# A two-block kernel in one program: in the first tile, two transposes of k and three blocks of w_out's roundings change their places

## The chip, the cores and the metric

The kernel runs on one core of a Trainium2 chip. The time is the device time of that core in microseconds (us), as the median of the runs. TensorE is PE in the profile (its weight loads are PEld), VectorE is DVE, ScalarE is ACT, GpSimd is POOL, and SyncE, which here only issues DMAs, is SP. ACT and POOL issue DMAs too.

## The reference

Two blocks follow each other. The first is a retention block with decay over 8 batches, 8 heads, 576 positions and 64 columns a head; the second is a gated feed-forward block (SwiGLU).

```
scores = q @ k.T / 8                           # per batch and head, 576 x 576
x      = (scores * decay[head]) @ v            # decay: gamma_h ** (i - j) for i >= j, else 0
x      = x.transpose(0, 2, 1, 3).reshape(4608, 512)
g      = x @ w_gate                            # 512 x 1536
out    = (g * sigmoid(g) * (x @ w_val)) @ w_out   # w_out: 1536 x 512
```

## The kernel before

Attention is done in chunks of 64 positions, for pairs of heads: 8 batches of 4 pairs are 32 pairs, numbered through; HP is 4. The 4608 tokens are cut into a first tile of 512 tokens (tile 0) and four tiles of 1024. Tiles 1 to 4 multiply their matrices with a scheme of fewer block products and more block sums; the sums fall to DVE and POOL. Tile 0 multiplies plainly.

The order of each engine's instructions is the order in which the program writes them: a manual schedule holds for all five engines. So where a line stands in the program decides what waits behind what.

**Tile 0, up.** In `plan` (lines 1513 to 1547) twelve steps f = 0 to 11 make one block of 128 hidden columns each, by `up0(f, ...)` (859): 4 products with w_gate into one PSUM bank and 4 with w_val into a second, then a silu of the first on ACT (874) and a product of the two on DVE (875). Even steps use bankA and bankB, odd ones bankC and bankE. So step f+2 overwrites the banks that step f's silu and product read. The profile counts each fp32 matmul twice, so a step's bank is a row of x8.

**Weights.** They arrive as float64 and are made float32 in two halves per block. `load_w` (368) issues a load of 1 MB, the later ones on POOL's queue. `split(j)` (389) is two ACT instructions (398, 399) that split the halves' bits, into one of two pairs of buffers; `rounding(j)` (408) is two DVE instructions (415, 416) that put them together, and then issues `split(j + 1)`. A split after the second half of a block issues the load of the block three further on (402 to 406). The blocks' order is `order` (361): blocks 0 to 11 are w_gate and w_val in turn, blocks 12 to 17 are w_out, with 12 between 6 and 7, 13 between 8 and 9, and 14 between 10 and 11. `round_until(i)` (1515) puts all roundings up to block i into the plan. The blocks that step f needs are rounded two steps ahead; those of w_out are needed only by tile 0's down stage (`down0`, 880), after all steps.

**Ticks.** Between the steps stand ticks, one per pair of heads. `tick(t)` (787) writes PE's attention products for pairs t-1 and t-2 and then a list `pieces`: copies on ACT, x of pair t-2 on DVE or ACT, masks and states of pair t-1 on DVE, and last, from `transposes(t)` (455), the DVE transposes of q and of k of pair t (line 477, into qT and the single buffer kT). `end_masks` (691) ends the pieces of tick 6. Without `spread` a tick runs all its pieces at once; `go_on(n)` (839) runs the next n. Tick 5 stands behind step 3, tick 6 behind step 5, tick 7 behind step 7, ticks 8 and 9 behind steps 10 and 11. PE's products of tick t+1 read what the transposes of tick t made. `end_transposes` (680, two DVE instructions on line 682) prepares the rest of batch 0, which PE reads in tick 6 (688).

**Loads of q, k and v.** `load(t)` (255) issues 10 DMAs for a pair on SP's queue: k and v by tokens (290), q and k again for the transposes (299), 4 each. SP issues in order.

**After the steps** come tile 0's down stage, with ticks 10 to 13 and with the sums of w_out's blocks on DVE and POOL (904), stored by SP (974, named dn); then tile 1, in which POOL makes the weight sums (1061) that PE reads (1208).

Of the kernel before, what the change touches and what calls it, by code (L numbers as in the profile page):

```python
# [132 lines left out]
def kernel(  # L133
# [38 lines left out]
    HP = H // 2  # L172
# [71 lines left out]
    def whole(i):  # L244

        return HP <= i < needed(2) - 2
# [262 lines left out]
    def own_values(i, n=0):  # L509

        s, ret = st[i], places(i)[0]
        cs = [a + d for a in (1 - n, 5 - n) for d in (0, 2)] if whole(i) else range(0 if n else NC - 1)
        for c in cs:
            for hl in range(2):
                rows, at = chunk(i, hl, c)
                start = n == 0 and c in (cs[:2] if whole(i) else (0, 1))
                m = nc.tensor.matmul(value(i, hl, c), s["v"][rows, at], ret[rows, c % 2 if whole(i) else hl, c // 2],  # L517
                                     start=start, stop=start, skip_group_check=True)
        if n == 0:
            s["own"] = m  # L520

    def new_states(i):
        s = st[i]
        for c in range(NFULL):
            for r in range(2):
                for hl in range(2):
                    rows, at = chunk(i, hl, 2 * c + r)
                    nc.tensor.matmul(z[half[hl], r, c], s["kn"][chunk(i, hl, 2 * c + r)], s["v"][rows, at],  # L528
                                     start=True, stop=True, skip_group_check=True)

    def earlier_values(i):
        s, (_, ret_last, state) = st[i], places(i)

        wait = nc.tensor.nop()
        tc.add_manual_dep(wait.ins, s["own"].ins.name,
                          mybir.DependencyInfo(mybir.DependencyClass.Sync, mybir.DependencyReason.DATA), reason="row halves")
        own_values(i, 1)
        for hl in range(0 if i < HP else 2):
            rows, at = chunk(i, hl, NC - 1)
            nc.tensor.matmul(xr[half[hl]], s["v"][rows, at], ret_last[rows],  # L540
                             start=False, stop=False, skip_group_check=True)
        for c in (1, 3, 4, 6, 5, 7, 2, 8) if whole(i) else range(1, NC - (i < HP)):
            for hl in range(2):
                nc.tensor.matmul(xr[half[hl]] if c + 1 == NC else value(i, hl, c), state[half[hl], c, :],  # L544
                                 s["qT"][half[hl], ts(c, L)], start=False, stop=True, skip_group_check=True)
# [140 lines left out]
    def end_scores():  # L686
        for n, x, hl in ends:
            nc.tensor.matmul(end_at[x][half[hl ^ x], n], end_k[half[hl], 2 * x + n], end_q[half[hl], 2 * x + n],
                             start=False, stop=True, skip_group_check=True)
# [5 lines left out]
    def end_own(x):  # L695
        for n, _, hl in [e for e in ends if e[1] == x]:
            rows = half[hl ^ x]
            m = nc.tensor.matmul(end_at[x][half[hl ^ x], n], end_v[rows, 2 * x + n], end_ret[rows, 2 * x + n],
                                 start=False, stop=False, skip_group_check=True)
        return m  # L700

    def end_earlier():
        for n, x, hl in ends:
            nc.tensor.matmul(end_at[x][half[hl ^ x], n], end_states[half[hl], 2 * x + n], end_q[half[hl], 2 * x + n],
                             start=False, stop=True, skip_group_check=True)
# [7 lines left out]
    pieces = []  # L713
# [73 lines left out]
    def tick(t, lo=HP, hi=NP, spread=False, then=None):  # L787
        go_on(len(pieces))
        if lo <= t - 2 < hi:
            own_values(t - 2)  # L790
            if t == HP + 3:
                st[t - 2]["own"] = end_own(1)
        if lo <= t - 1 < hi:
            new_states(t - 1)
        if lo <= t - 2 < hi:
            earlier_values(t - 2)
            if t == HP + 3:
                end_own(0)
                end_earlier()
        if lo <= t - 1 < hi:  # L800
            scores(t - 1, t - 2 < lo)
            if t == HP + 2:
                end_scores()
        if lo <= t - 1 < hi and whole(t - 2) and not whole(t - 1):
            decay(slice(0, H), slice(0, H), half[1])
        copies, *masks = masked(t - 1) if lo <= t - 1 < hi else (lambda: None,)
        keys, *new = transposes(t) if lo <= t < hi else (lambda: None,)
        outputs = to_x(t - 2)[0] if lo <= t - 2 < hi else lambda: None
        late = needed(1) - 4 <= t < needed(1) - 2 or light(t - 2)
        if late and masks:  # L810
            own, (last, pairs, odd, evens) = masks
            pieces.extend([lambda: (copies(), own(), outputs()), [last, pairs, odd, lambda: (evens(), keys())]])
        elif late:
            pieces.append(lambda: (copies(), outputs(), keys()))
        else:
            pieces.extend([lambda: (copies(), keys()), outputs])
            for own, (last, pairs, *rest_of) in [masks] if masks else []:
                pieces.extend([own, [lambda: (last(), pairs()), *rest_of]])
        if then and new:
            pieces.extend(new[:-1])  # L820
            pieces.append(lambda: (new[-1](), then()))
        else:
            pieces.extend(new)
            pieces.extend([then] if then else [])
        if t == HP + 2:
            pieces.append(end_masks)
        if t == HP + 3:
            pieces.append(end_to_x)
        if not spread:
            go_on(len(pieces))  # L830
# [8 lines left out]
    def go_on(n):  # L839
        for _ in range(min(n, len(pieces))):  # L840
            while part_on():
                pass
# [16 lines left out]
    def up0(f, chunks, parts=range(2)):  # L859

        pair = banks[2 * (f % 2) : 2 * (f % 2) + 2]
        for gv in parts:
            bank = pair[gv]
            for c in chunks:
                w = w_up[:, f // 4, gv, f % 4, c // 2, (c % 2) * P : (c % 2 + 1) * P]
                if f == 2 or f == 3 and gv == 0:
                    for m in range(2):
                        nc.tensor.matmul(bank[:, ts(m, TB)], w, xs[0][:, c, ts(m, TB)],
                                         start=(c == 0 and m == 0), stop=(c == HP - 1), skip_group_check=True)
                    continue  # L870
                last_up[0] = nc.tensor.matmul(bank, w, xs[0][:, c, :], start=(c == 0), stop=(c == HP - 1))  # L871
        if HP - 1 in chunks:
            s = io[:, (f % 2) * T0 : (f % 2 + 1) * T0]
            nc.scalar.activation(out=s, in_=pair[0], func=AF.Silu)
            nc.vector.tensor_tensor(out=hid0[f], in0=pair[1], in1=s, op=ALU.mult)
# [629 lines left out]
    FIRST = needed(1) - 2  # L1505
# [7 lines left out]
    plan = []  # L1513

    def round_until(i):
        while todo and order.index(i) >= todo[0]:
            m = todo.pop(0)
            plan.extend(lambda j=j: rounding(j, j != 2 * len(order) - 3) for j in (2 * m, 2 * m + 1))

    round_until(3)  # L1520
    tick_at = {2: 4, 3: 5, 5: 6, 7: 7, 10: 8, 11: 9}
    for f in range(2, NF):
        if f == 3:
            plan.append(lambda: tick(HP, HP, FIRST))
        round_until({4: 12, 6: 13, 8: 14, 9: 15, 10: 16, 11: 17}.get(f, f + 2))
        last_half = plan.pop() if f + 1 == NF else None
        plan.append(lambda f=f: up0(f, range(HP)))
        if last_half:
            plan.append(last_half)
        if f + 2 == NF:  # L1530
            plan.append(lambda: split(2 * len(order) - 2))
        if f + 1 == NF:
            plan.append(lambda: pool_places.extend(wide_places))
            plan.append(negate)
        if f - 1 in tick_at and f < 7:
            plan.append(lambda t=tick_at[f - 1]: next_load(t))
        if f in tick_at and f > 2:
            plan.append(lambda t=tick_at[f]: tick(t, HP, FIRST))
            if tick_at[f] == HP + 1:
                plan.append(end_transposes)  # L1540
        if f in (7, 10):
            if f == 10:
                plan.append(lambda: next_load(9))
            plan.append(lambda t=tick_at[f]: next_load(t))
# [3 lines left out]
    tick_at = {1: 10, 3: 11, 6: 12, 8: 13}  # L1548
# [89 lines left out]
```

## Time and profile before

| what | value |
|---|---|
| runs before | 1015.73 us median; 1012.75, 1015.73, 1017.21 |
| profiled execution, its own time | 1016.05 us |
| its span in the profile | 1014.3 us |
| granted TensorE clock, mean | 0.998 |
| PE busy | 1003.5 us |
| DVE busy | 721.5 us |
| POOL busy | 576.7 us |
| ACT busy | 285.7 us |
| DMA | 194.44 MB, 192 GB/s mean |

The page gives shares of the whole span. The views used below go closer: the table by stage gives, for a stretch of time, each engine's busy time with its instructions in brackets, the granted clock and the DMA share; the timeline gives each instruction's start, its length, its engine and line, what it writes and reads, and in square brackets how long its engine stood idle before it and what ended that; the chain of waits follows the work that ended last back through what released it. The queue shares list the packets, the megabytes and the share of the 16 DMA engines of each DMA queue: q0 carries POOL's loads, q1 what SP issues.

### The profile page before, as it was taken

Reading aid. Unit: us, or ns where it says so; the run is one execution under the profiler, and the core shown is the slowest. Engines: PE = TensorE matmul, PEld = TensorE weight load, DVE = VectorE, ACT = ScalarE, POOL = GpSimd, SP = SyncE. Lnnn points to the kernel's source line nnn. Section 1 sums busy time; section 2 is a strip of 40 time slices with the busy share of each in tenths; the row PEclk is TensorE's granted clock in tenths of the full one; section 3 lists DMA queues with packets and bytes.
Section 4 is the critical chain, followed back from the end, with each engine's and each line's share of the span. In section 5 each row is a group of like instructions: output and inputs, shape, how many; then the busy total and the mean of one; then the engine's idle time right before and its main releaser. Section 6 shows DMA issues by size and latency. Waiting matters only on the chain.

```text
span 1014.3 us, 21283 instructions
## 1 busy us (share of the span) xinstructions
PE 1003.5 (99%) x8302; PEld 827.2 (82%) x8302; DVE 721.5 (71%) x1210; ACT 285.7 (28%) x636; POOL 576.7 (57%) x611
## 2 busy tenths in 40 slices
PE   8989999999999999999999999999999999999998
PEld 6644555888888888888888888888888888888887
DVE  5549889578886675977778678866575767566745
ACT  5535632132423322133322202233320012233110
POOL 3511348989577218575564157746672586566614
PEclk9999999999999999999999999999999999999999
DMA  9999977788788886857668786434454454445553
GB/s 235 272 221 300 200 202 276 199 227 224 147 232 248 211 185 218 206 170 199 185 180 226 172 200 191 163 126 166 161 172 141 147 195 146 145 152 186 176 162 103
DMA packets 273933, 194.44 MB, mean 192 GB/s; under 512 B 212329, under 2 KB 241897, under 8 KB 273833
## 3 DMA queue, kind: packets, MB, share of 16 engines
q1 hardware_dynamic: 249448, 99.49, 39.9%
q10 hardware_dynamic: 20208, 79.57, 24.1%
q0 software_dynamic: 4176, 14.03, 4.2%
q8 instruction: 66, 1.08, 0.5%
q14 instruction: 35, 0.28, 0.1%
HBM read 154.11 MB, written 38.93 MB: 190 GB/s over the span
## 4 chain that ended last, share of the span: by engine, by line
PE 93%; SPq 3%; DMA 2%; ACT 0%; issue 0%; DVE 0%; ACTq 0%; DVEq 0%
PE bankB L1208 12%; PE bankE L1208 12%; PE bankA L1208 12%; PE bankC L1208 12%; PE bankE L1415 7%; PE bankC L1415 7%; PE bankB L1415 7%; PE bankA L1415 6%; SPq L299 2%; PE outer L517 2%; PE inner L1208 2%; PE outer L1208 2%; PE outer L544 1%; PE inner L558 1%; PE bankA L871 1%; PE inner L528 1%
## 5 line engine op out<-in xcount | busy, mean ns | idle before, releaser
L1061 POOL TENSOR_TENSOR rest<-rest 128x512 f32<-128x512 f32 (+1 forms) x143 | 150.9, 1066 | 158.0 <-DVE rest L1061 110.2
L1223 POOL TENSOR_TENSOR arena<-rest,io 128x256 f32<-128x256 f32 x168 | 124.2, 753 | 78.2 <-ACT io L1222 70.6
L1222 ACT ACTIVATE io<-rest 128x256 f32<-128x256 f32 x192 | 79.2, 417 | 210.6 <-DVE rest L1061 132.5
L1208 PE MATMUL bankB<-rest,arena 128*128 128x256 f32 x428 | 110.1, 381 | 0.0
L1208 PE MATMUL bankE<-rest,arena 128*128 128x256 f32 x424 | 107.8, 379 | 0.0
L1061 DVE TENSOR_TENSOR rest<-bankC,rest 128x512 f32<-128x512 f32 x112 | 75.8, 684 | 40.1 <-PE bankC L1208 23.1
L1208 PE MATMUL bankA<-rest,arena 128*128 128x256 f32 x408 | 104.0, 379 | 0.0
L1061 DVE TENSOR_TENSOR rest<-bankB,rest 128x512 f32<-128x512 f32 x110 | 74.7, 685 | 41.2 <-PE bankB L1208 29.8
L1061 DVE TENSOR_TENSOR rest<-bankA,rest 128x512 f32<-128x512 f32 x112 | 75.9, 685 | 38.1 <-PE bankA L1208 19.3
L1061 DVE TENSOR_TENSOR rest<-bankE,rest 128x512 f32<-128x512 f32 x116 | 78.5, 685 | 30.0 <-PE bankE L1208 19.0
L1208 PE MATMUL bankC<-rest,arena 128*128 128x256 f32 x368 | 94.2, 380 | 0.0
L1208 PEld LDWEIGHTS bankB<-rest,arena 128*128 128x128 f32 x428 | 80.7, 190 | 11.9 <-DVE rest L1061 0.9
L1208 PEld LDWEIGHTS bankE<-rest,arena 128*128 128x128 f32 x424 | 80.5, 190 | 11.0
L1208 PEld LDWEIGHTS bankA<-rest,arena 128*128 128x128 f32 x408 | 77.5, 190 | 10.6
L1208 PEld LDWEIGHTS bankC<-rest,arena 128*128 128x128 f32 x368 | 69.4, 190 | 10.1 <-DVE rest L1061 0.6
L1061 POOL TENSOR_TENSOR arena<-arena 128x256 f32<-128x256 f32 (+1 forms) x76 | 70.8, 954 | 8.9 <-PE bankC L1208 7.6
L1415 PE MATMUL bankE<-arena 128*128 128x256 f32 x264 | 61.0, 381 | 0.0
L1415 PE MATMUL bankC<-arena 128*128 128x256 f32 x264 | 60.9, 380 | 0.0
L1415 PEld LDWEIGHTS bankE<-arena 128*128 128x128 f32 x264 | 49.8, 190 | 7.0 <-POOL arena L904 0.2
L1415 PEld LDWEIGHTS bankC<-arena 128*128 128x128 f32 x264 | 49.9, 190 | 6.9
L1415 PE MATMUL bankB<-arena 128*128 128x256 f32 x240 | 55.3, 380 | 0.0
L1415 PE MATMUL bankA<-arena 128*128 128x256 f32 x228 | 52.8, 380 | 0.2 <-issue 0.2
(294 smaller groups left out, 1883.5 us busy)
## 6 DMA issues: line engine op xcount, KB each, us to landing
arena<-up ACTq DMA_DIRECT2D x60, 896.0 KB, 4.6
arena<-dn ACTq DMA_DIRECT2D x60, 384.0 KB, 3.7
arena<-dn SPq DMA_DIRECT2D x44, 384.0 KB, 3.9
out_dram<-rest SPq DMA_DIRECT2D x31, 256.0 KB, 2.4
qk<-in_q_dram SPq DMA_DIRECT2D x108, 72.0 KB, 4.1
qk<-in_k_dram SPq DMA_DIRECT2D x108, 72.0 KB, 3.3
dn<-rest SPq DMA_DIRECT2D x26, 256.0 KB, 2.4
up<-arena SPq DMA_DIRECT2D x13, 512.0 KB, 3.5
```

The costliest lines, as they stand in the source:

```text
L299: queue.dma_start(out=qk[a * SQ : (a + 1) * SQ, n], in_=src[b, 2 * p + a // 2, :, (a % 2) * SQ : (a % 2 + 1) * SQ].rearrange("(j t) d -> t ...
L517: m = nc.tensor.matmul(value(i, hl, c), s["v"][rows, at], ret[rows, c % 2 if whole(i) else hl, c // 2], start=start, stop=start, skip_grou ...
L528: nc.tensor.matmul(z[half[hl], r, c], s["kn"][chunk(i, hl, 2 * c + r)], s["v"][rows, at], start=True, stop=True, skip_group_check=True)
L544: nc.tensor.matmul(xr[half[hl]] if c + 1 == NC else value(i, hl, c), state[half[hl], c, :], s["qT"][half[hl], ts(c, L)], start=False, stop ...
L558: nc.tensor.matmul(sc[chunk(i, hl, 2 * c + r)[0], r if whole(i) else hl, c], kT[half[hl], at], qT[half[hl], at], start=True, stop=True, sk ...
L871: last_up[0] = nc.tensor.matmul(bank, w, xs[0][:, c, :], start=(c == 0), stop=(c == HP - 1))
L1061: eng.tensor_tensor(out=out, in0=a, in1=b, op=ALU.add if sign > 0 else ALU.subtract)
L1208: m = nc.tensor.matmul(b[:, g * TB : (g + 1) * TB], w[:, g], x, start=(opens and g == 0), stop=True, skip_group_check=True)
L1222: nc.scalar.activation(out=s, in_=src[:, 0:TB], func=AF.Silu)
L1223: (nc.vector if busy and o != 2 and qd + 1 < NQ else nc.gpsimd).tensor_tensor(out=hid[:, qd, 2 * H + h, 2 * T + t], in0=src[:, TB : 2 * TB ...
L1415: nc.tensor.matmul(b[:, m * TB : (m + 1) * TB], lhs[:, qd, ts(m, P)], w[:, qd], start=(opens and qd == 0 and m == 0), stop=(qd == NQ - 1), ...
```

## The change

The change touches only the list `plan` of tile 0's steps. Three things move; no instruction is added or taken away.

- After tick 5, the transpose of k of pair 5 is held back. At step 4 the two roundings of the next w_gate block (6) come first, then that transpose, then `end_transposes`, then `up0(4)`.
- After tick 6, the transpose of k of pair 6 and `end_masks` are held back in the same way, behind the two roundings of block 8 at step 6.
- At steps 4, 6 and 8 the two roundings of the w_out block (12, 13, 14), with the splits that they issue, are written behind `up0(f)`, and so behind the step's silu on ACT and its product on DVE. Before, they stood ahead of it. At step 6 block 8, and at step 8 block 10, stay ahead.

```diff
     for f in range(2, NF):
         if f == 3:
             plan.append(lambda: tick(HP, HP, FIRST))
-        round_until({4: 12, 6: 13, 8: 14, 9: 15, 10: 16, 11: 17}.get(f, f + 2))
+        round_until({4: 6, 6: 8, 8: 10, 9: 15, 10: 16, 11: 17}.get(f, f + 2))
+        if f - 1 in (3, 5):
+            plan.append(lambda: go_on(len(pieces)))
+            if f == 4:
+                plan.append(end_transposes)
         last_half = plan.pop() if f + 1 == NF else None
         plan.append(lambda f=f: up0(f, range(HP)))
+        if f in (4, 6, 8):
+            round_until({4: 12, 6: 13, 8: 14}[f])
         if last_half:
             plan.append(last_half)
...
         if f in tick_at and f > 2:
-            plan.append(lambda t=tick_at[f]: tick(t, HP, FIRST))
-            if tick_at[f] == HP + 1:
-                plan.append(end_transposes)
+            plan.append(lambda t=tick_at[f]: tick(t, HP, FIRST, t in (5, 6)))
+            if tick_at[f] in (5, 6):
+                plan.append(lambda t=tick_at[f]: go_on(len(pieces) - t + 4))
```

In the built program the orders of PE, POOL and SP are the same as before; those of DVE and ACT differ at the three places.

## The prediction

> **What bounds the kernel now.** I read the page first: the busy shares, then the chain that ended last.
>
> ```profile
> PE 1003.5 (99%) x8302; PEld 827.2 (82%) x8302; DVE 721.5 (71%) x1210; ACT 285.7 (28%) x636; POOL 576.7 (57%) x611
> ...
> PE 93%; SPq 3%; DMA 2%; ACT 0%; issue 0%; DVE 0%; ACTq 0%; DVEq 0%
> ```
>
> TensorE (PE) is busy 1003.5 of 1014.3 us. A change of order that leaves its work alone can only win idle time of PE, or a lower clock. So I asked for PE's idle stretches: one is 4.09 us long, no other is over 0.4 us. It lies where the diff works. The table by stage shows it (time, then busy us of PE, PEld, DVE, ACT, POOL, the granted clock, DMA share, GB/s):
>
> ```profile
> 68.00:70.00 2.00, 1.96 (x116) 1.81 (x108) 1.79 (x5) 0.00 (x0) 0.00 (x0) 1.00 0.92 169
> 70.00:72.00 2.00, 0.12 (x9) 0.00 (x0) 1.86 (x4) 1.94 (x4) 0.00 (x0) 1.00 0.51 80
> 72.00:74.00 2.00, 0.00 (x0) 0.00 (x0) 1.73 (x4) 2.00 (x4) 0.70 (x1) 1.00 0.81 132
> 74.00:76.00 2.00, 1.78 (x2) 0.81 (x3) 1.91 (x5) 1.96 (x4) 0.42 (x1) 0.57 0.84 217
> ```
>
> PE stands from 70.13 to 74.22, and when it resumes its granted clock is about half. The timeline of the four engines says why:
>
> ```profile
> 74.22 5.40 PE L871 MATMUL bankA<-rest,arena 128*128 128x512 f32 x8 [4.09 <-ACT io L874]
> 79.45 3.60 PE L871 MATMUL bankB<-rest,arena 128*128 128x512 f32 x8
> ...
> 56.65 0.77 DVE L477 STREAM_TRANSPOSE qT<-qk 128x576 f32<-128x576 f32 x1
> 68.18 0.78 DVE L477 STREAM_TRANSPOSE kT<-qk 128x576 f32<-128x576 f32 x1 [10.75 <-DMA qk<-in_k_dram]
> 68.88 0.73 DVE L682 STREAM_TRANSPOSE rest<-rest 128x256 f32<-128x256 f32 x2
> ...
> 55.14 0.67 ACT L399 ACTIVATE rest<-rest 128x512 int32<-128x512 uint32 x1
> 70.00 0.68 ACT L398 ACTIVATE rest<-rest 128x512 f32<-128x512 f32 x1 [14.19 <-DVE arena L415]
> 73.59 0.58 ACT L874 ACTIVATE io<-bankA 128x512 f32<-128x512 f32 x1
> ...
> 72.81 0.70 POOL L381 DMA_DIRECT2D rest<-in_moe_w_out_dram  x1 [15.95 <-ACT rest L399]
> ```
>
> Read from the bottom of the cause: VectorE (DVE) stands 10.75 us at the transpose of k of pair 5, because k has not landed. The roundings stand behind it, the splits of ScalarE (ACT) wait for the roundings, and the silu of step f=4 stands behind three splits. Its input was ready by 57, when PE's bankA run of f=4 ended. PE needs that bankA for f=6. The chain of waits agrees: it holds the transfer of k from 55.75 to 68.15, then the two splits, the silu, and PE at 74.22.
>
> **Part 1, f=4.** DVE: the two roundings of the next w_gate block (L415 0.42 and L416 0.69, one pair every 1.17 us) move ahead of the transpose of k, into the 10.75 us hole: 57.4 to 59.7. The two of w_out move behind the product L875 of f=4. ACT: silu f=4 now stands behind one split, not three. That split needs its w_out block (issued 52.93; such loads land 7.0 us after issue, so about 59.9) and takes 1.2 us; silu ends near 61.5. bankA is then free long before PE wants it at 70.13. Were nothing else changed, PE would win 4.09 us, and the slow run too: bankA to bankB takes 5.23 us there against 3.54 after the tick at 92.88, so 1.69. **Together 5.78 us.** What is late next in that case is bankB of f=6, whose weights are the third rounding behind the transpose: 68.96 + 0.65 (L682) + 0.6 (L875) + 3 x 1.17 = 73.7, and PE gets there at 73.56: nothing.
>
> **What it triggers.** POOL's and SP's orders are unchanged, but POOL's next load of w_out (1 MB) is released by the end of the second split, which now runs behind silu f=4: near 62.6 instead of 72.52. So the load goes out at 62.9, not 72.81; it moved its bulk from 75.2 (2.4 us after issue), so now from about 65.3, just behind the three loads already queued. What a weight load does to SP's queue of small packets is in the queue shares; first 56 to 64.5, with weight loads, then 70 to 74, without:
>
> ```profile
> q0 software_dynamic: 705, 2.76, 91.2%
> q1 hardware_dynamic: 1391, 0.17, 14.2%
> ```
> ```profile
> q1 hardware_dynamic: 3386, 0.42, 66.1%
> ```
>
> With a load in flight SP's queue moves 164 packets per us; alone it moves 846 even at two thirds of the engines. A load of 1.05 MB holds the engines 8.5 x 0.912 x 1.05 / 2.76 = 2.9 us. The last packets of k of pair 5 go out between 65 and 67 (landing 68.15). The load now falls on them. Bounds: 0 if it starts after 67, 2.9 if it starts before the tail; the estimate of 65.3 is nearest to the second, less the few packets that pass: **I take 2.7 us.** The transpose then starts at 70.9 and ends at 71.65; PE's scores, 69.01 before, start at 71.7; the rest of that tick takes 1.12, so f=6 starts at 72.8: 1.4 us won of 4.09. PE's idle time is 2.7 us, now inside the tick. Does the clock fall? The rows granted 1.00 through 74 and 0.57 only from 74, that is 4.1 us after PE stopped; a stand of 0.38 us (19.4) left no mark. 2.7 us ends before the point at which the one dip came: I take none, so 1.69 is won. PE leaves f=6 **3.1 us early** (bounds 1.4 and 5.78).
>
> The Trainium skill, "TensorE: Matmul & The Clock Gate", section "HAM oscillation — how this bites in real kernels", asks for no PE-idle gaps over about 3.4 us, and Part 1 of that page has the clock follow a free-running window. By the limit 2.7 us stays warm, as I take it; by an unlucky window the dip comes all the same, the fourth rival below. This trace's one dip, after 4.09 us, fits both; no row tests 2.7.
>
> **Parts 2 and 3, f=6 and f=8.** No PE idle time follows them in the trace, so they win nothing by themselves; they take cover away and give some. At f=6 the transpose of k of pair 6 and the masks L693 move behind two roundings, 2.33 us. L693 ended at 83.9 and PE's tick began at 89.84. DVE's own position: from the transpose at 71.65 through L682, L875 and four roundings to L875 of f=5 it arrives at 77.6, against 77.32, so +0.3. L693 then ends at 86.5, PE arrives at 86.7: cover 0.2 us, price 0; with k on time PE comes 5.78 sooner and DVE 2.4 sooner, and the cover is the same 0.2. At f=8 silu comes 2.3 us sooner, which covers PE's bankA of f=10 (silu ended 103.90, PE 106.72). DVE waits for PE at 113.86 (0.77) and 115.60 (1.05); these go, so DVE is 1.5 early. States for the tick at 132.61 were done at 131.36, cover 1.25: PE keeps 1.5 + 1.25 = 2.75 us.
>
> **Tile 1.** Here POOL makes operands and is busy without a break from 167.23 to 212.8.
>
> ```profile
> 196.06 2.51 POOL L1061 TENSOR_TENSOR arena<-arena 128x512 f32<-128x512 f32 x2
> ...
> 198.95 1.89 PE L1208 MATMUL bankC<-x_odd,arena 128*128 128x256 f32 x8
> ```
>
> POOL's second sum ends at 198.57; PE's run that reads it reaches those weights at 199.38: 0.8 us of cover; at 238.23 it is 0.7 (POOL's row of 235.00). PE keeps only 0.7 plus what POOL itself gains. POOL's chain hangs on SP, whose issues follow each other unbroken from 57 to 133.8, where the first dn store lets POOL go on at 138.93. SP gains the DMA time that stood empty: 34% of 70 to 74, 1.4 us, which the earlier load now fills; bounds 0 and 2. I take 1.5, a little more for 74 to 75. **So 0.7 + 1.5 = 2.2 us survive**, and from there PE carries them to the end. The profiled execution took 1016.05 us (span 1014.3): 1016.05 - 2.2 = **1013.8**. The median of the runs, 1015.73, is 0.3 lower; the sum would be 1013.5 by it.
>
> **Rivals.**
> - *The whole stall goes.* The load comes too late to touch k and POOL follows PE: 5.78, so 1010.3. For: only a 2 us tail of k is exposed. Against: POOL's 0.7 us of cover. 10%.
> - *POOL gives it all back.* SP and POOL gain nothing: 0.7 survives, 1015.3. For: SP's rows near 130 look bound by their own 0.54 us per issue. 20%.
> - *Slower: the load starves SP.* The 1 MB at 65 delays k, then q and k of pairs 6 and 7 behind it in SP's queue, and SP reaches its first dn store after 133.8. It decides from 0.7 us late on, POOL's cover in tile 1; 2 us late costs 2 - 0.7 = 1.3, whatever PE won before: 1017.4. Against: the DMA work is the same in sum, and an empty stretch is filled. 13%.
> - *The clock falls in the tick.* 2.7 us of idle lies nearer to 4.09, which had a dip, than to 0.38. Then 1.69 is paid again, PE wins 1.4, under what POOL lets through: 1014.6. Against: no dip before 74. 12%.
> - *The change does nothing it says.* Excluded: DVE's and ACT's orders differ as described, PE's does not.
>
> **How the numbers follow.** The forecast has 45%; the rivals have 10, 20, 13 and 12. About 0.5% (5.1 us) is what a measurement of this kernel can tell from no change; its three runs lie 4.5 us apart. Faster by that needs 1010.65 or less: the first rival, at 1010.3, in most cases, 0.08. Slower by it needs 1020.8: only a much longer delay than the one priced in the slower rival, 0.05. The rest, 0.87, is within. The range runs from the first rival's 1010.3 to the slower one's 1017.4, rounded to 1017.5.
>
> **What would show it.** Right: silu f=4 near 61; the w_out load issued near 63; the transpose of k of pair 5 at 70 to 71.5; f=6 on PE near 72.8 with no clock below 1.00; PE's lead 2.7 us at 165 and near 2 at 240, with new waits of PE for POOL between. Wrong: the transpose still at 68.2 (first rival), or a lead at 240 below 1, or a dip of the clock at 72.

## The result

The changed kernel is slower: 1020.61 us median (1017.51 to 1021.78, 17 runs) against 1017.01 for the kernel before in the same comparison (1012.75 to 1021.59, 17 runs), a ratio of 1.0032 with a 95% interval of 1.0020 to 1.0045. The forecast was 1013.8, its range ended at 1017.5, and its sign was wrong. The profiled execution took 1021.78 us (span 1020.1), the longest of the 17; before it was 1016.05 (span 1014.3).

The page first, its busy line and the shares of the chain that ended last:

```profile
PE 1004.5 (98%) x8302; PEld 827.5 (81%) x8302; DVE 719.5 (71%) x1210; ACT 285.2 (28%) x636; POOL 576.6 (57%) x611
...
PE 87%; DMA 6%; issue 4%; SPq 1%; POOL 0%; ACT 0%; DVE 0%; ACTq 0%; POOLq 0%
```

PE is busy 1.0 us more than before and the span is 5.8 longer, so PE waits more. In the chain PE has fallen from 93 to 87% and DMA risen from 2 to 6%: it now passes through transfers. The table by stage (columns as before) shows where:

```profile
70.00:72.00 2.00, 2.00 (x6) 0.80 (x6) 1.85 (x4) 1.90 (x4) 0.00 (x0) 1.00 1.26 239
72.00:74.00 2.00, 2.00 (x6) 0.91 (x5) 1.73 (x4) 2.00 (x5) 0.77 (x1) 1.00 0.65 83
74.00:76.00 2.00, 2.00 (x6) 0.92 (x5) 1.91 (x6) 2.00 (x6) 0.00 (x0) 1.00 0.96 149
...
102.00:104.00 2.00, 0.00 (x0) 0.00 (x0) 1.93 (x6) 0.25 (x1) 0.00 (x0) 1.00 1.11 212
104.00:106.00 2.00, 0.31 (x1) 0.30 (x2) 1.75 (x4) 1.94 (x4) 0.00 (x0) 1.00 0.87 125
106.00:108.00 2.00, 2.00 (x3) 0.68 (x2) 1.95 (x4) 1.92 (x4) 0.71 (x1) 0.53 0.81 144
```

The hole at 70 to 74 is filled, at full clock. The same hole now stands at 101 to 105.7, and the same half clock behind it. The timeline shows that part 1 did all that was asked of it, and then the same chain once more, one pair of heads later:

```profile
61.67 0.58 ACT L874 ACTIVATE io<-bankA 128x512 f32<-128x512 f32 x1
...
63.66 0.70 POOL L381 DMA_DIRECT2D rest<-in_moe_w_out_dram  x1 [6.80 <-ACT rest L399]
...
67.64 0.78 DVE L477 STREAM_TRANSPOSE kT<-qk 128x576 f32<-128x576 f32 x1 [8.01 <-DMA qk<-in_k_dram]
...
69.72 3.70 PE L871 MATMUL bankA<-rest,arena 128*128 128x512 f32 x8
...
101.67 0.78 DVE L477 STREAM_TRANSPOSE kT<-qk 128x576 f32<-128x576 f32 x1 [7.05 <-DMA qk<-in_k_dram]
...
103.75 0.67 ACT L398 ACTIVATE rest<-rest 128x512 f32<-128x512 f32 x1 [13.09 <-DVE arena L415]
...
105.06 0.58 ACT L874 ACTIVATE io<-bankA 128x512 f32<-128x512 f32 x1
...
105.69 5.40 PE L871 MATMUL bankA<-rest,arena 128*128 128x512 f32 x8 [5.00 <-ACT io L874]
```

The first four rows are f=4 and f=6: silu at 61.67, the load of w_out 13 at 63.66, k of pair 5 at 67.64 (68.18 before), PE at 69.72, without a stand (74.22 before). The last four are pair 7, whose transpose the change does not hold back: DVE stands 7.05 us for k, the roundings of block 10 stand behind it, a split behind them, the silu of f=8 behind that, and PE waits 5.00 us for bankA of f=10. Before, this transpose was at 97.64 and waited 0.15 us, and PE did not stand:

```profile
97.64 0.78 DVE L477 STREAM_TRANSPOSE kT<-qk 128x576 f32<-128x576 f32 x1 [0.15 <-DMA qk<-in_k_dram]
...
103.31 0.58 ACT L874 ACTIVATE io<-bankA 128x512 f32<-128x512 f32 x1
...
106.72 3.60 PE L871 MATMUL bankA<-rest,arena 128*128 128x512 f32 x8
```

PE's lead over the kernel before, from the starts of the same rows in the two traces, adds up: 74.22 - 69.72 = 4.5 at f=6; 6.19 from f=8 on, with the half-clock run gone; 1.03 at f=10 (5.16 lost, of which the stand is 5.00); -0.77 at its bankB (1.8 lost in a half-clock run, as at f=6 before); -1.70 and -2.94 in f=11 (stands of 0.86 and 1.09, the first of them behind a split that waited 4.00 us for a w_out block, whose load went out at 107.05, behind a split that had stood behind the same k; 102.56 before); -4.47 after tick 10 (1.29); and a last 1.25 at 434.37, where PE waits for a transfer in tile 1. With it the sum is -5.7; the spans differ by 5.8.

### The profile page after: what moved, and what is told of

Its sections match the earlier page's. It is cut to its first block, busy times and chain, and to the rows that moved or that the text cites. A ratio compares the mean times of both kernels' runs of the same rounds, so it can differ in the third digit from the quotient of the medians.

```text
span 1020.1 us, 21281 instructions
## 1 busy us (share of the span) xinstructions
PE 1004.5 (98%) x8302; PEld 827.5 (81%) x8302; DVE 719.5 (71%) x1210; ACT 285.2 (28%) x636; POOL 576.6 (57%) x611
## 4 chain that ended last, share of the span: by engine, by line
PE 87%; DMA 6%; issue 4%; SPq 1%; POOL 0%; ACT 0%; DVE 0%; ACTq 0%; POOLq 0%
PE bankB L1208 12%; PE bankE L1208 12%; PE bankA L1208 12%; PE bankC L1208 11%; PE bankE L1415 7%; PE bankC L1415 7%; PE bankB L1415 7%; PE bankA L1415 6%; DMA rest<-in_moe_w_out_dram 2%; DMA rest<-in_moe_w_gate_dram 2%; PE outer L1208 2%; PE inner L1208 2%; PE outer L517 2%; PE outer L544 1%; PE inner L558 1%
```

## The experiments

The theory was that transfers do it: the change lets weight loads run ahead, the small packets of q and k on SP's queue fall behind them, and k of pair 7 lands late (T1, T1b). The rivals: the stall only moves on because PE arrives sooner (T2); or w_out's roundings behind the silu do the harm (T3). Each kernel has 6 to 12 runs beside 17 to 35 runs of the kernel before (the change 17 and 17). Each run lists its mean granted clock. One half-clock run of 3.41 us makes it about 0.998 (0.5 x 3.41 / 1015), so the last column counts the runs at 0.998 or less: those in which PE stood long enough to lose its clock, wherever that was. Only one run of each kernel was profiled, so the rows below are those of single runs; the change's is the longest of its 17.

| kernel | median us | before, beside it | ratio [95%] | runs with a half-clock run |
|---|---|---|---|---|
| the change | 1020.61 | 1017.01 | 1.0032 [1.0020, 1.0045] | 16 of 17 |
| late_w13 | 1019.97 | 1016.10 | 1.0036 [1.0023, 1.0048] | 8 of 8 |
| hold_7 | 1019.48 | 1016.10 | 1.0018 [0.9997, 1.0039] | 7 of 12 |
| hold_only | 1019.97 | 1016.10 | 1.0036 [1.0023, 1.0048] | 7 of 7 |
| wout_only | 1015.21 | 1016.10 | 0.9994 [0.9979, 1.0009] | 3 of 12 |
| paced | 1016.03 | 1015.39 | 1.0007 [0.9991, 1.0023] | 4 of 12 |
| light_13 | 1016.46 | 1015.39 | 1.0002 [0.9986, 1.0018] | 2 of 12 |
| hold_5 | 1013.14 | 1015.39 | 0.9988 [0.9975, 1.0001] | 0 of 11 |
| hold_6 | 1016.73 | 1015.39 | 1.0016 [1.0003, 1.0029] | 8 of 11 |
| part_1 | 1016.48 | 1015.67 | 0.9997 [0.9977, 1.0016] | 6 of 12 |
| no_hold_6 | 1017.42 | 1015.67 | 1.0007 [0.9988, 1.0026] | 4 of 12 |
| paced_45 | 1014.59 | 1015.67 | 0.9992 [0.9976, 1.0007] | 2 of 12 |
| light_14 | 1014.04 | 1015.66 | 0.9989 [0.9975, 1.0004] | 1 of 12 |
| hold_5_paced | 1021.18 | 1015.66 | 1.0055 [1.0038, 1.0072] | 6 of 6 |

The kernel before had such a run in 19 of 26, 25 of 35, 17 of 28 and 14 of 17 of its runs in the four groups beside the experiments: in its profile it is the stall at f=6. Its median differs between groups (1015.39 to 1017.01), so the ratios are what compares. The recorded ratio is not the quotient of the two medians beside it: for hold_5 the medians give 0.9978, the ratio is 0.9988.

### late_w13: one load held back

```diff
     # split(): the load of block 13 is kept, not issued
-            if j == 3:
+            if j == 3 or order[m + RAWS + (m < RAWS)] == 13:
     # plan, f == 4, behind round_until(12): POOL waits for that rounding, then issues it
+            plan.append(late_load)
```

> The changed kernel, but the load of w_out block 13 is held until the second rounding of w_out block 12 is done (near 71.5 us; it went out at 63.66 with the change and at 72.81 before). Nothing else moves. Theory T1 (the earlier weight load delays SP's queue, so that k of pair 7 lands late and the stall comes back at f=10): k of pair 7 is read by VectorE near 98 instead of 101.7, TensorE's gap before f=10 falls from 5.0 to 1 us or less, no half-clock run follows, about 1016 us against 1020.6. T1b (all weight loads run ahead, since the whole pipeline does, and this one is not special): k of pair 7 at 100 or later, gap 3 to 5 us, 1019 or more. Rival T2 (the stall moves only because TensorE arrives sooner; transfers have no part in it): k of pair 7 and the gap as with the change, 1020.6.

The load went out at 70.81 instead of 63.66. k of pair 7 was read at 100.21, PE's gap before f=10 was 3.25 us with a half-clock run, and the time stayed. T1 in its first form, the early issue of w_out 13 alone, falls.

### hold_7: the transpose of pair 7 held as well

```diff
-        if f - 1 in (3, 5):
+        if f - 1 in (3, 5, 7):
             plan.append(lambda: go_on(len(pieces)))
... (left out here; the loads behind tick 7 are written behind this place too)
-            plan.append(lambda t=tick_at[f]: tick(t, HP, FIRST, t in (5, 6)))
+            plan.append(lambda t=tick_at[f]: tick(t, HP, FIRST, t in (5, 6, 7)))
```

> The change, and the transpose of k of pair 7 is held behind the roundings of step 8's w_gate block too, as the change does for pairs 5 and 6. T1: k of pair 7 still lands near 101.5, but the silu of f=8 no longer stands behind it (near 98 instead of 105.06), TensorE's 5.0 us gap before f=10 and its half-clock run go (6.7 us of them), and TensorE waits next for the loads behind or for pair 8: 1014 to 1016 us. T2 (each such hold only moves the wait to the next place): a gap of 3 to 5 us at tick 8 or at f=11, 1019 to 1021.

The silu of f=8 came at 96.86, and bankA of f=10 did not wait. But k was read still later, at 103.67, and on DVE the product of f=8 and then three pairs of roundings stand behind it. PE's bankB of f=10 needs the third pair (ended 109.32) and waits instead. PE's rows of this kernel:

```profile
109.38 5.40 PE L871 MATMUL bankB<-rest,arena 128*128 128x512 f32 x8 [3.15 <-DVE arena L416]
...
129.07 0.56 PE L558 MATMUL inner<-qT,kT 64*64 64x64 f32 x19 [2.30 <-issue]
```

In this trace the hold moved the wait to the next place that hangs on the same k; five of 12 runs have no half-clock run. The time is as T2 had it, but k itself moved too, which T2 does not explain.

### hold_only and wout_only: the two halves of the change

```diff
     # hold_only: the holds of the change; w_out's roundings ahead of the silu, as before
+        if f in (4, 6, 8):
+            round_until({4: 12, 6: 13, 8: 14}[f])
         last_half = plan.pop() if f + 1 == NF else None
         plan.append(lambda f=f: up0(f, range(HP)))
-        if f in (4, 6, 8):
-            round_until({4: 12, 6: 13, 8: 14}[f])
     # wout_only: the reverse; ticks 5 and 6 run their pieces at once, as before
```

> Only the transposes of k of pairs 5 and 6 are held; the roundings of w_out stand ahead of the step's silu as before. The silu of f=4 then stands behind the splits that wait for the transpose's successors, near 71, so TensorE keeps about 2 us of its gap at f=6 (half-clock run perhaps gone), and the load of w_out 13 goes out near 70 instead of 63.66. T1: k of pair 7 lands near 98, no gap over 1 us at f=10, 1013 to 1016 us. T2: what is won at f=6 is lost at f=10: 1017 to 1018. Rival T3 (what costs is the roundings of w_out behind the silu, parts 1 to 3 alike): faster than before, 1013 to 1015, with the weight loads in time.

> Only the roundings of w_out stand behind the silu; the transposes stay where they were. The silu of f=4 then stands behind the transpose at 68.2 and one split pair, near 71.3, and the load of w_out 13 goes out near 73 as before. T1: k of pair 7 lands as before (near 98), TensorE wins about 2 us at f=6 and keeps most of it, 1014 to 1016. T3 (the roundings of w_out behind the silu delay splits and loads of the last blocks and the silu of f=9): new waits of TensorE between 105 and 120 of 1 to 3 us, 1018 to 1021.

The holds alone make the whole loss (k of pair 7 at 101.01, gap 6.12 us). w_out's roundings alone cost nothing that shows (the interval holds 1): T3 falls. For hold_only T1 and T2 had both forecast less, 1018 at most. In wout_only PE stood 1.81 us at f=6 instead of 4.09 and k of pair 7 was read at 97.16 without a wait.

### hold_5 and hold_6: the two holds, each alone

```diff
     # hold_5, on the kernel before (left out here: the table of round_until; tick 5 stops short of the transpose of k)
+        if f == 4:
+            plan.append(lambda: go_on(len(pieces)))
+            plan.append(end_transposes)
+            round_until(12)
     # hold_6, on the kernel before (left out here likewise, for tick 6)
+        if f == 6:
+            plan.append(lambda: go_on(len(pieces)))
+            round_until(13)
```

> Before, with one change: the transpose of k of pair 5 (and the two of the last rows) held behind the roundings of step 4's w_gate block; w_out's roundings and pair 6's transpose as before. Both holds together, without the w_out part, gave 1020.0 and a gap of 6.1 us at f=10. T1b: the roundings run from 57, the loads of w_out 13, val 9 and gate 10 go out 4 to 11 us sooner, k of pair 7 is read near 100, gap 3 to 6 us, 1018.5 to 1020. If it is the hold of pair 6 that does the harm: 1013 to 1015 here.

> Before, with one change: the transpose of k of pair 6 (and the end rows' masks) held behind the roundings of step 6's w_gate block. The old gap at f=6 stays. T1b: the loads up to 79.7 are as before, k of pair 7 within 1 us of before (97.6 to 98.6), 1015.5 to 1017.5, no difference. If this hold does the harm: k of pair 7 at 100 or later, a gap at f=10 beside the one at f=6, 1019 or more.

The expectation for hold_5 by T1b was a miss: by its median it is the fastest kernel of the study, without a single half-clock run, and k of pair 7 was read at 98.10. That was not in time, though:

```profile
98.10 0.78 DVE L477 STREAM_TRANSPOSE kT<-qk 128x576 f32<-128x576 f32 x1 [2.98 <-DMA qk<-in_k_dram]
```

PE stood 1.86 us at f=6 and 1.16 us at f=10, both at full clock. hold_6 alone is a little slower than before; its k of pair 7, at 99.71, came later than expected. Together (hold_only) they lose 4 us. So it is the hold of pair 6, on top of a pipeline that already runs early, that does the harm here.

### no_hold_6 and part_1: the change without that hold, and its first place alone

```diff
     # no_hold_6, on the change
-        if f - 1 in (3, 5):
+        if f == 4:
             plan.append(lambda: go_on(len(pieces)))
-            if f == 4:
-                plan.append(end_transposes)
+            plan.append(end_transposes)
     # and tick 6 runs its pieces at once, as before
     # part_1: besides, w_out 13 and 14 rounded ahead of the silu, as before
```

> The change without its hold of pair 6's transpose; the rest as in the change. Pair 5's hold alone gave 1013.1 and pair 6's added to it 1020.0. If pair 6's hold is what brings the loads of w_out 14, val 11 and w_out 15 forward and k of pair 7 back (T1b): k of pair 7 read 2 to 3 us sooner than 101.7, gap at f=10 of 0 to 2 us, 1012 to 1016. If w_out's roundings behind the silu together with pair 5's hold do the same harm: 1018 to 1021.

> Only the place at f=4 is changed: pair 5's transpose held behind the roundings of w_gate, w_out 12's roundings behind the silu of f=4. All of the 4.09 us gap and the half-clock run at f=6 can be won. T1b (the loads behind f=6 set what SP's queue gets before k of pair 7): the loads of w_out 14 to w_out 15 go out 1 to 3 us later than with the whole change, k of pair 7 is read between 97 and 99, few runs show a half-clock run, 1011 to 1014. If the early load of w_out 13 (near 63) is enough by itself: k of pair 7 near 101, most runs with a half-clock run, 1017 to 1020.

Both missed their expectations (1012 to 1016, 1011 to 1014) and did not meet the rival's. Without the hold 12 runs lie between 1012.4 and 1020.57, in part_1 between 1012.06 and 1020.97, with a half-clock run in 4 and 6 of them instead of nearly all. It looks like a race for k of pair 7 that is lost in part of the runs. That is argued, since no lost run has a trace; in the two profiles it was won. DVE's row for k of pair 6 in no_hold_6, and those for k of pairs 6 and 7 in part_1:

```profile
82.54 0.78 DVE L477 STREAM_TRANSPOSE kT<-qk 128x576 f32<-128x576 f32 x1 [2.61 <-DMA qk<-in_k_dram]
```
```profile
81.00 0.78 DVE L477 STREAM_TRANSPOSE kT<-qk 128x576 f32<-128x576 f32 x1 [3.30 <-DMA qk<-in_k_dram]
94.60 0.77 DVE L477 STREAM_TRANSPOSE qT<-qk 128x576 f32<-128x576 f32 x1
95.30 0.74 DVE L477 STREAM_TRANSPOSE kT<-qk 128x576 f32<-128x576 f32 x1
```

Here DVE waits for k of pair 6 with the roundings of block 8 behind it. While it waits, no split follows, so no weight load is released: the load of w_out 14 went out at 87.45 and 85.40, against 83.51 with the hold. In these two traces a wait for a small transfer paced the large ones, and the hold took that pace away. That is read from the rows; it is not the only pace, since before and in hold_5 k of pair 6 was there without a wait.

### paced and paced_45: the loads held back, nothing else

```diff
     # paced_45: the loads of blocks 14 and 15 are kept, and issued on POOL behind a wait
+        if f == 7:
+            plan.append(lambda: late_load(silu_of[7]))     # w_out 14, behind the silu of f=7
+        if f == 8:
+            plan.append(lambda: late_load(last_up[0]))     # w_out 15, behind PE's f=8
     # paced: block 13 too, as in late_w13
```

In both the load of block 11 goes ahead of that of w_out 14 (the lines that keep the loads, and the instructions that they wait for, are left out here).

> The changed kernel with three weight loads held back to about their old times: w_out 13 until the last rounding of w_out 12 (near 71.5; 63.66 with the change, 72.81 before), w_out 14 until the silu of f=7 is done (near 88.5; 83.51 and 87.15), w_out 15 until TensorE ends f=8 (near 94; 90.95 and 95.70). Holding only w_out 13 left k of pair 7 at 100.21 and a gap of 3.25 us, so T1 in its first form (this one load) falls. T1b (all loads run ahead, and together they keep SP's queue of q and k back): k of pair 7 near 98, gap before f=10 of 1.5 us or less, no half-clock run, 1015 to 1016.5. T2 (transfers have no part, the stall moves with the order of VectorE): k of pair 7 at 100 or later, gap of 3 us or more, 1019 to 1020.5.

> The change with only the loads of w_out 14 (until the silu of f=7) and w_out 15 (until TensorE ends f=8) held back; w_out 13 goes out near 63 as in the change. Holding 13 alone gave 1020.0, holding 13, 14 and 15 gave 1016.0. If the loads right ahead of k of pair 7 decide: k of pair 7 at 97 to 99, half-clock runs in a third of the runs or fewer, 1015 to 1017. If 13 and the others add up: 1017.5 to 1019. T2 (order alone): 1020.

DVE's, ACT's and PE's orders are those of the change; only when POOL issues the loads of 1 MB, and the order of two of them, differs (in paced_45 block 11 at 85.58, w_out 14 at 87.47, w_out 15 at 94.33; the change had w_out 14 at 83.51, block 11 at 87.10, w_out 15 at 90.95). The loss is gone: 1014.59 against 1020.61, and 2 half-clock runs of 12, though PE is as early as in the change (f=8 at 86.65 and 86.69). paced, with w_out 13 held as well, lies at 1016.03, with 4 half-clock runs of 12 where none was expected. The queue shares from 76 to 88 (packets, MB, share of the engines), first of the change, then of paced_45:

```profile
q0 software_dynamic: 672, 2.62, 64.3%
q1 hardware_dynamic: 4704, 0.89, 49.2%
```
```profile
q1 hardware_dynamic: 7944, 1.29, 69.2%
q0 software_dynamic: 329, 1.22, 33.4%
```

With one load less in flight SP's queue moves 7944 packets instead of 4704 in the same 12 us. SP's own rows show what that does to its issues of q and k of pair 7, again the change and then paced_45:

```profile
80.43 6.00 SPq L299 DMA_DIRECT2D qk<-in_q_dram  x4
86.46 6.21 SPq L299 DMA_DIRECT2D qk<-in_k_dram  x4
92.79 3.83 SPq L290 DMA_DIRECT2D kn<-in_k_dram  x1
```
```profile
79.14 5.79 SPq L299 DMA_DIRECT2D qk<-in_q_dram  x4
84.97 3.47 SPq L299 DMA_DIRECT2D qk<-in_k_dram  x4
88.56 0.43 SPq L290 DMA_DIRECT2D kn<-in_k_dram  x1
```

SP ends the issue of k 4.2 us sooner (88.56 against 92.79) and k is read 5.0 us sooner (96.64). PE then runs through:

```profile
100.67 3.70 PE L871 MATMUL bankA<-rest,arena 128*128 128x512 f32 x8
105.02 3.70 PE L871 MATMUL bankB<-rest,arena 128*128 128x512 f32 x8 [0.65 <-DVE arena L416]
```

This pair of kernels does not show where the change falls behind the kernel before. From 76 to 88 the kernel before had no more room than the change: 748 packets on POOL's queue and 4542 on SP's. The difference lies ahead of that, from 68 to 76 (first before, then the change):

```profile
q1 hardware_dynamic: 6005, 0.91, 65.1%
q0 software_dynamic: 65, 0.27, 11.1%
```
```profile
q0 software_dynamic: 307, 1.19, 50.1%
q1 hardware_dynamic: 3674, 0.47, 46.6%
```

Before, hardly any weight load moved there, since w_out 13 went out only at 72.81. With the change it and block 9 (72.90) fall there, and SP begins to issue q of pair 7 at 80.43 instead of 74.35 and k at 86.46 instead of 81.79. So SP falls behind from 68 to 76, and the loads behind keep it from making that good; with two of them held it does. late_w13 does not clear this stretch either: with w_out 13 at 70.81 and block 9 at 71.50, POOL's queue moves 278 packets in it.

### light_13 and light_14: the bytes of one load taken away

```diff
+            rows = slice(0, P // 8 if i == 14 else P)      # light_13: i == 13
-            queue.dma_start(out=dst.rearrange("p (f c) n -> p f (c n)", f=2), in_=src)
+            queue.dma_start(out=dst[rows].rearrange("p (f c) n -> p f (c n)", f=2), in_=src[rows])
```

> The changed kernel, but the load of w_out 13 moves only 16 of its 128 partitions (the rest of that block keeps old data, so an eighth of the block is what the reference has): 0.92 MB, some 2.5 us of the DMA engines, are gone, and no instruction moves. T1b: k of pair 7 is read 2 to 3 us sooner than with the change (near 99), TensorE's gap before f=10 falls from 5.0 to 2 to 3 us, 1016 to 1018. T2: k of pair 7 and the gap as with the change, 1020.6.

> The change, but the load of w_out 14 (issued 83.51) moves only 16 of its 128 partitions, so most of that block keeps old data; every instruction and its order is as in the change. If the bytes in the DMA engines are what keeps k of pair 7 back (T1b): k of pair 7 read at 97 to 99.5, half-clock runs in a third of the runs or fewer, 1014 to 1017. If it is POOL's order or the time of the splits: as the change, 1020, nearly all runs with a half-clock run.

Every instruction stands where the change has it; seven eighths of one block do not travel. light_13 gives 1016.46 with 2 half-clock runs of 12, so the bytes of w_out 13 count, although its later issue alone won nothing (its profile fell on the longest of its runs, with k of pair 7 at 100.91, and shows no gain); light_14 gives 1014.04 with 1 of 12. In light_14's profile (its lines are numbered one higher) k of pair 7 comes at 95.46 and PE does not stop:

```profile
95.46 0.78 DVE L478 STREAM_TRANSPOSE kT<-qk 128x576 f32<-128x576 f32 x1 [2.13 <-DMA qk<-in_k_dram]
```
```profile
98.18 3.60 PE L872 MATMUL bankE<-rest,arena 128*128 128x512 f32 x8
101.61 3.60 PE L872 MATMUL bankA<-rest,arena 128*128 128x512 f32 x8
105.04 3.60 PE L872 MATMUL bankB<-rest,arena 128*128 128x512 f32 x8
```

So it is what the weight loads move through the shared DMA engines, not the order of any engine: T2 falls.

### hold_5_paced: the best version with its loads held

```diff
     # hold_5, and the two late_load calls of paced_45
```

> Pair 5's hold alone (1013.1), with the loads of w_out 14 and w_out 15 held back as in the paced version. T1b: k of pair 7 keeps a little more room than with pair 5's hold alone (98.1), no half-clock run, 1011.5 to 1013.5. If the held loads then come too late for their own splits: silu of f=9 after 112, waits of TensorE at f=11, 1014 to 1017.

The worst kernel of the study, by the second of the two mechanisms and beyond the 1017 that it was given. k of pair 7 was in time (92.80, no wait). But with w_out 14 rounded ahead of `up0(8)` the load of w_out 16 is written ahead of the held one of w_out 15, which stands behind it on POOL until 99.38; a split waits for it, the silu of f=9 behind the split comes at 112.96, and PE loses at f=11 (PE's row, then ACT's):

```profile
113.58 5.26 PE L871 MATMUL bankC<-rest,arena 128*128 128x512 f32 x8 [3.43 <-ACT io L874]
```
```profile
109.59 0.68 ACT L398 ACTIVATE rest<-rest 128x512 f32<-128x512 f32 x1 [7.74 <-DMA rest<-in_moe_w_out_dram]
```

Held too long (w_out 15 went out at 100.07, with paced_45 at 94.33) a weight load costs as much as when it goes too early.

## Why the prediction was wrong

- **What bounds the kernel; 5.78 us at stake.** Right. PE was 6.19 early at f=8; the half-clock run was worth 1.69.
- **The load of w_out 13 delays k of pair 5 by 2.7 us.** Wrong. The time of issue was right (63.66; 62.9 forecast), but k of pair 5 was read at 67.64, no later than before, and the whole 5.8 us were won by f=8, which was the first rival's condition. The term was mis-sized at the start of the load's bulk, put at 65.3: POOL's queue moved 20 packets from 66 to 68 and 173 from 68 to 70, when k of pair 5 had been read. What the load did slow was SP's work for pairs 6 and 7; from 68 to 70 (1839 packets on SP's queue before):

```profile
q0 software_dynamic: 173, 0.71, 94.0%
q1 hardware_dynamic: 122, 0.03, 9.7%
```

- **Parts 2 and 3 win and cost nothing; price 0 at f=6. This is the step that failed.** It counted only DVE's and PE's own cover at the next tick. That sum held: PE did not stand at tick 7. It did not ask what the roundings that are moved ahead release: splits, and by them three loads of 1 MB (w_out 14, block 11, w_out 15) that go out at 83.51, 87.10 and 90.95. The kernel before had them at 87.15, 89.89 and 95.70, and no_hold_6, the change without this hold, at 87.45, 89.99 and 93.86. With the hold they travel beside q and k of pair 7, whose issue was late already. The row that spoke was in the trace: k of pair 7 was read with a wait of 0.15 us before, so it had no cover at all, and the silu of f=8 stood behind it by the same chain that the change broke up for pair 5. hold_only shows the price with this hold (1019.97, ratio 1.0036), hold_5 without it (1013.14, ratio 0.9988), paced_45 and light_14 that it is paid in DMA time.
- **"Silu comes 2.3 us sooner" at f=8.** The size was right, the start was not: the silu came 3.39 us behind the transpose of k of pair 7 instead of 5.67, 2.28 sooner, but that transpose came 4.03 later, so the silu was 1.75 late (105.06 against 103.31). w_out's roundings behind the silu are harmless as such (wout_only).
- **The slower rival, the load starves SP (13%).** Its mechanism, q and k of pairs 6 and 7 late behind the load, was right; its place and price were not. It was priced at SP's first dn store and POOL's cover in tile 1, 1.3 us; it was paid at f=10, with the clock, at 5.0 + 1.7.
- **Tile 1 lets 2.2 us through.** Near in size, and by luck, for two kernels in which PE came early: PE was 5.0 ahead at f=11 in paced_45 and 5.1 in light_14, and their spans end 2.1 and 2.7 ahead of before (1012.2 and 1011.6 against 1014.3). The terms of the sum, POOL's cover and SP's gain, are not what decided. The lead goes at f=11 (1.71 in paced_45) or at tick 10 (1.35 in light_14, PE's row at 129.03), and in tile 1 near 285 (1.18 and 0.63), where PE waits for a tick's operands; POOL's sums at 199 stopped nothing. By the medians these two kernels win less, 1.1 and 1.6 us.
- **The clock.** Once PE was running, no stand between 0.4 and 4.1 us was in the trace before. Now: stands of 1.81, 1.71 and 2.30 us left the clock alone, stands of 3.15, 3.25 and 3.43 us had a half-clock run of 3.41 us, so the 2.7 that was forecast lies between, and no run tests it. The Trainium skill, "TensorE: Matmul & The Clock Gate", section "HAM oscillation — how this bites in real kernels", gives about 3.4 us as the limit; the two shortest stands with a dip lie under it, so the limit is not sharp here. By Part 1 of the same page of the Trainium skill the clock follows a free-running window. The granted clocks agree: each half-clock run starts a whole number of 3.413 us after the full clock was first granted, 20 of them (68.267 us) before and 29 (98.987 us) in the change, wherever the stand itself began.

The Trainium skill, "DMA: Bandwidth & Descriptors", section "Queues, rings and completion order", says that each DMA engine takes turns between its queues by whole packets. The packet counts of 76 to 88 agree with it as far as they go: fewer packets of q0, more of q1. No run here measures the turns themselves.

What stays open: why none of the 11 runs of hold_5 has a half-clock run but six of 12 of part_1 do, though the two kernels differ by w_out 12's roundings alone. PE comes to f=6 at 72.25 in hold_5 and at 69.67 in part_1, so the less hurried kernel fits the theory; no run isolates it. Nor does one separate how much of the loss is due to the loads from 68 to 76 and how much to those behind them. The best version, hold_5, lies under both kernels by its median, and from the kernel before it isn't separated (0.9975 to 1.0001).

## What to carry to other kernels

A wait can be a throttle. Before moving work out of a wait, list what that work releases, DMAs above all, and look in the trace for the next transfer that lands with no cover: it is there that the win can be lost. When a stall goes, run the same chain for the next item of the loop. Here that chain had the same shape and no room (k of pair 7 was waited for by 0.15 us), and the stall only moved.

## What the runs showed of the hardware

- A megabyte in small packets takes more of the DMA engines than one in large packets: from 76 to 88 in the change, 0.89 MB in 4704 packets on SP's queue took 49.2% of the 16 engines, 2.62 MB in 672 packets on POOL's took 64.3%. In paced_45 1.40 MB less on POOL's queue went with 3240 more packets, 0.40 MB, on SP's.
- The half clock comes in pieces of 3.41 us: 3.41 us behind stands of 3.15 to 5.00 us in the change, late_w13, hold_7, light_13 and hold_5_paced; 6.83 us, two pieces, in hold_only (stand of 6.12 us) and hold_6 (3.63 us), where the first piece began within the stand itself.
- The same program's runs spread over 8.9 us in part_1 (1012.06 to 1020.97) and over 4.3 us in hold_5 (1010.6 to 1014.93) and in the change (1017.51 to 1021.78). That the wide spread is a race won in some runs and lost in others is argued, not shown.
